# Fused window attention and MLP on one core: first loads and w_out products re-placed, and 512-token blocks in slots 72 to 135

## The chip, the core and the metric

The kernel runs on one core of one Trainium2 chip. The metric is the device time of one execution in microseconds. Four runs of the kernel before the change took 308.22 to 309.41 us, median 309.25 us. The profile shown here belongs to one execution that took 309.22 us.

## The reference

Two stages follow each other. First, attention with a window of 32 positions to each side, for 8 batches, 8 heads, 576 positions and a head dimension of 64:

```python
scores = scale * np.matmul(q, k.transpose(0, 1, 3, 2))
mask = np.abs(pos[:, None] - pos[None, :]) <= window
attn = softmax(np.where(mask, scores, -1e9))        # over the last axis
x = np.matmul(attn, v).transpose(0, 2, 1, 3).reshape(B * S, H * D)
```

This gives x with 4608 tokens (8 x 576) of 512 values. Second, an MLP with a smooth ReLU, w_in being 512 x 2048 and w_out 2048 x 512:

```python
h = x @ w_in
g = np.where(h >= 1, h, np.where(h <= -1, 0.0, (h + 1) ** 2 / 4))
out = g @ w_out
```

Inputs and output are float32 in HBM. The kernel computes with bf16 operands and float32 sums.

## The kernel before, in words

**Slots.** The MLP is cut into 18 blocks of 256 tokens (`TB`), and each block into 8 steps of 256 columns of w_in. One block and one step make one *slot*, so there are 144 slots, numbered `a`, and 8 more in which only products with w_out are left. The loop at L491 writes out the order of the work by hand; there is no scheduler (`tc.manual_schedule()`). An engine executes its instructions in the order in which this loop emits them.

One slot emits, in this order:

- `project` (L483 to L488): 8 matmuls on TensorE, each with a moving operand of 256 tokens of xT and 128 x 128 weights of w_in, into one PSUM tile `hp` of 2 x 256. Two such tiles exist (pool `ps_h`), so the matmuls of slot a wait until slot a-2 has let its tile go. Slot 6 alone takes its tile from another pool.
- ScalarE: `rr` = relu(0.5 h + 0.5) from `hp` (L519).
- VectorE: `mx` = max(hp, rr) (L526), and then `g` = min(rr, 1) * mx (L527), which goes as bf16 to a tile `gT` of this block. After `mx` the `hp` tile is free. In the slots of `two_on_act` (1 and 7 to 12) ScalarE makes the square, and VectorE reads `hp` in its single step (L524), so there the tile is free only after `g`.
- `flush` and `run(a)`: a session of the attention, if the table `sl` (L409) puts one into this slot. A session has `sums` (L265; products of probabilities with v and with ones on TensorE, then Ln and Exp on ScalarE at L299 and L300 for the reciprocal, and in the next slot a multiplication on VectorE that writes xT, L305 or L308) and `scores` or `scores8` (products of q and k on TensorE, Exp on ScalarE at L235 or L260, mask on VectorE at L201).
- w_out products: from slot 18 on `quarter` (L425), 4 matmuls with a moving operand of 512 columns of w_out (L445), on values of `gT` that are 8 slots old. Four quarters finish 128 tokens; ScalarE copies them to `osb` (L450) and SP's queue stores them. The first two blocks are done by `pair` (L453; 8 matmuls with 256 columns each, L461), in the slots that the list `pairs` (L379) names. The last 128 tokens go in two halves (L434).

**Sessions and blocks.** Batch b fills tokens 576 b to 576 b + 575 of x. A batch takes five sessions: two for its tokens 0 to 223, two for 224 to 479, and a tail session for 480 to 575. Each must be done before the first block that reads its tokens. xT is a ring of four batches.

**First loads.** POOL's queue carries all loads but the first q. They come in the order in which L118 to L157 emit them, and the loads go round over eight semaphores: the ninth waits on POOL until the first has landed, and so on. w_in comes in pieces of 256 columns, halved by rows (h = 0, 1), except for columns 1024 to 1535, which come as one piece per half. Slot a of block 0 reads columns 256 a to 256 a + 255 of both halves. `step` is made on POOL (L131) and gives, on VectorE, the identity for the transposes and the band (L138 to L140). The mask tiles are copied on POOL (L151 to L154) between the last piece of w_in and the second piece of w_out. VectorE uses them in slot 16 for the first time.

Of the kernel before, what the change touches and what calls it, by code (L numbers as in the profile page):

```python
# [7 lines left out]
FP = mybir.dt.float32  # L8
BF = mybir.dt.bfloat16
# [5 lines left out]
def kernel(  # L15
# [19 lines left out]
    nc = tc.nc  # L35
    B, H, S, D = q.shape
    NT, DM, DFF = out.shape[0], 512, 2048
# [4 lines left out]
    TAIL = S - MAIN  # L42
    RING = 4 * S
    PAD = 32
    LONG = 2

    const = ctx.enter_context(tc.tile_pool(name="const", bufs=1))
# [2 lines left out]
    ptp = ctx.enter_context(tc.tile_pool(name="ptp", bufs=2))  # L50
    smp = ctx.enter_context(tc.tile_pool(name="smp", bufs=2))
    ewp = ctx.enter_context(tc.tile_pool(name="ewp", bufs=3))
    gtp = ctx.enter_context(tc.tile_pool(name="gtp", bufs=3))
    osp = ctx.enter_context(tc.tile_pool(name="osp", bufs=3))
    ps_h = ctx.enter_context(tc.tile_pool(name="ps_h", bufs=2, space=bass.MemoryType.PSUM))
    ps_s = ctx.enter_context(tc.tile_pool(name="ps_s", bufs=1, space=bass.MemoryType.PSUM))
# [11 lines left out]
    w_in = const.tile([128, 4, DFF], BF, name="w_in")  # L68
    w_out = const.tile([128, 16, DM], BF, name="w_out")
    xT = const.tile([128, NY, RING], BF, name="xT")  # L70
    qTs = [const.tile([128, PAD + NY * S], BF, name=f"qT{i}") for i in range(3)]

    ctx.enter_context(tc.manual_schedule())
# [27 lines left out]
    def load_v(b, n):  # L101
        if b not in vn:
            vn[b] = nat.tile([128, 2 * NC, 2, D], BF, name="vn", tag="vn", bufs=3)
        h, a = divmod(n, 2)
        y = NY * h + 2 * a
        nc.gpsimd.dma_start(out=vn[b][64 * a:64 * a + 64, :, h], in_=v[b, y:y + 2].rearrange("y s d -> (y s) d")  # L106
                            .rearrange("(c r) d -> r c d", r=64))
# [14 lines left out]
    for h in range(2):  # L122
# [5 lines left out]

    step = early.tile([128, 257], BF, name="step")
    V.memset(step, 0.0)  # L130
    P.affine_select(out=step, in_=step, compare_op=ALU.is_ge, fill=-1.0, base=-65, channel_multiplier=-1,  # L131
                    pattern=[[1, 257]])
    for n in range(4):
        load_v(0, n)
    V.memset(ones, 1.0)
    for t in qTs:
# [5 lines left out]
    def put(todo):  # L142
        for fn, *x in todo:
            fn(*x)

    w = [(load_w_in, c, c + 256, h) for c in range(0, 1024, 256) for h in range(2)]
    w += [(load_w_in, 1024, 1536, h) for h in range(2)]
    w += [(load_w_in, c, c + 256, h) for c in range(1536, DFF, 256) for h in range(2)]
    put(w[:4] + [(load_half, 1, t, h) for t in range(2) for h in range(2)] + w[4:12])
    put([(load_w_out, 0, 0, 4)] + w[12:])  # L150
    P.tensor_copy(band[HD[1], 0:128], band[HD[1], 64:192])  # L151
    for m, n, x in ((mask4, 8, 128), (mask8, 4, TAIL)):
        P.tensor_copy(m.rearrange("p (n j) -> p n j", n=n),
                      band[:, :x].rearrange("p (n j) -> p n j", n=1).to_broadcast([128, n, x]))  # L154
    put([(load_w_out, 0, k, k + 4) for k in range(4, 16, 4)] + [(load_rows, 1, t) for t in range(2)])
    put([(load_v, 1, n) for n in range(4)] + [(load_w_out, 1, 8 * n, 8 * n + 8) for n in range(2)])
    put([(load_nat, 2, t) for t in range(2)] + [(load_v, 2, n) for n in range(4)])  # L157


# [156 lines left out]
    TB = 256  # L316
# [59 lines left out]

    NB = NT // TB
    NF = DFF // 256
    pairs = [(6, 0), (7, 1), (9, 2), (10, 3), (11, 4), (12, 5), (15, 6), (15, 8), (16, 7), (17, 9)]  # L379
    two_on_act = (1, 7, 8, 9, 10, 11, 12)  # L380
    ev = {}

# [23 lines left out]
        at(a, seq[2 + n][0])  # L406
    for n, a in enumerate((18, 20, 26.5, 28)):
        at(a, seq[3 + n][1])
    sl = [30, 32, 35, 39, 42, 45, 49, 52, 56, 59, 62, 65, 69, 73, 77, 81, 84, 88, 92]  # L409
    sl += [96, 99, 103, 106, 110, 113, 116, 120, 124, 128]  # L410
    for n, a in enumerate(sl):
        at(a, seq[6 + n][0], seq[7 + n][1] if n < len(sl) - 1 else None)
    for t in range(2):
# [6 lines left out]
        for t in range(2):  # L420
            xps.setdefault(a + 6 + 2 * t, []).append((b, t))

    gT, op = {}, {}

    def quarter(x):  # L425

        tt, ff = divmod(x, 4)
        if tt == NT // 128 - 1:
            half, n = divmod(ff, 2)
            if n == 0:  # L430
                op[tt] = ps_o.tile([128, 256], FP, name="op", tag="op")
            cols = slice(256 * half, 256 * half + 256)
            for j in range(NF * n, NF * n + NF):
                nc.tensor.matmul(op[tt], gT[tt // 2][:, j, 128 * (tt % 2):128 * (tt % 2) + 128], w_out[:, j, cols],  # L434
                                 start=j == 0, stop=j == 2 * NF - 1)
            if n:
                osb = osp.tile([128, 256], FP, name="osb")
                A.copy(osb, op[tt])
                nc.sync.dma_start(out=out[128 * tt:128 * tt + 128, cols], in_=osb)
            return  # L440
        if tt not in op:
            op[tt] = ps_o.tile([128, DM], FP, name="op", tag="op"), []
        o, done = op[tt]
        for j in range(4 * ff, 4 * ff + 4):
            nc.tensor.matmul(o, gT[tt // 2][:, j, 128 * (tt % 2):128 * (tt % 2) + 128], w_out[:, j],  # L445
                             start=not done, stop=len(done) == 2 * NF - 1, skip_group_check=True)
            done.append(j)
        if len(done) == 2 * NF:
            osb = osp.tile([128, DM], FP, name="osb")
            A.copy(osb, o)  # L450
            nc.sync.dma_start(out=out[128 * tt:128 * tt + 128, :], in_=osb)

    def pair(x):  # L453

        half, p, g = x // 8, x % 8 // 4, x % 4
        if (half, p) not in op:
            op[half, p] = ps_o.tile([128, 2, 256], FP, name="op", tag="op"), []
        o, done = op[half, p]
        for tt in range(2):
            for j in range(4 * g, 4 * g + 4):  # L460
                nc.tensor.matmul(o[:, tt], gT[p][:, j, 128 * tt:128 * tt + 128], w_out[:, j, 256 * half:256 * half + 256],  # L461
                                 start=not done, stop=len(done) == 4 * NF - 1, skip_group_check=True)
                done.append(j)
        if len(done) == 4 * NF:
            osb = osp.tile([128, DM], FP, name="osb")
            A.copy(osb, o.rearrange("p t f -> p (t f)"))
            nc.sync.dma_start(out=out[256 * p:256 * p + 256, 256 * half:256 * half + 256]
                              .rearrange("(t p) f -> p t f", p=128), in_=osb.rearrange("p (t f) -> p t f", t=2))
# [14 lines left out]
    def project(hp, f, r0, todo, first, last):  # L483

        for n, (j, kk) in enumerate(todo):
            nc.tensor.matmul(hp[:, j], w_in[:, kk, 256 * f + 128 * j:256 * f + 128 * j + 128],  # L486
                             xT[:, kk, r0:r0 + TB], start=first and n == 0, stop=last and n == len(todo) - 1,
                             skip_group_check=True)  # L488

    hps = []  # L490
    for a in range(NF * NB + NF):  # L491
        t, f = divmod(a, NF)
        eng = None if a < 14 else V
        post = [x for n, x in pairs if n == a] + [a - NF] * (a >= 2 * NF + 2)
        for b, x in loads.get(a, []):
            if x < 2:
                load_nat(b, x)
            else:
                for n in range(4):
                    load_v(b, n)  # L500
        if a == 0 or a > 3:
            flush()
        if t < NB:
            if t not in gT:
                gT[t] = gtp.tile([128, 2 * NF, TB], BF, name="gT", tag="gT")
            r0 = TB * t % RING
            if a in (0,):
                hps = [ps_h.tile([128, 2, TB], FP, name="hp", tag="hp") for _ in range(2)]
                for y in range(2):
                    for n in range(2):  # L510
                        project(hps[n], f + n, r0, [(j, y + 2 * m) for j in range(2) for m in range(2)], y == 0, y == 1)
            elif not hps:
                pool, tag = (ps_o, "op") if a == 6 else (ps_h, "hp")
                hps = [pool.tile([128, 2, TB], FP, name="hp", tag=tag)]
                project(hps[0], f, r0, [(j, kk) for j in range(2) for kk in (0, 2, 1, 3)], True, True)
            hp = hps.pop(0)

            rr = ewp.tile([128, 2, TB], FP, name="rr")
            A.activation(rr, hp, AF.Relu, scale=0.5, bias=0.5)  # L519
            g = gT[t][:, 2 * f:2 * f + 2]  # L520
            mx = ewp.tile([128, 2, TB], FP, name="mx")
            if a in two_on_act:
                A.activation(mx, rr, AF.Square)  # L523
                V.scalar_tensor_tensor(g, hp, 1.0, mx, op0=ALU.max, op1=ALU.min)  # L524
            else:
                V.tensor_max(mx, hp, rr)  # L526
                V.scalar_tensor_tensor(g, rr, 1.0, mx, op0=ALU.min, op1=ALU.mult)  # L527
        flush()
        run(a)
        for x in post:  # L530
            (pair if x < 4 * 4 else quarter)(x)
        run(a + 0.5)
        for x in xps.get(a, []):
            xpose(*x)
# [30 lines left out]
```

## Time and profile before

| what | us |
|---|---|
| median of four runs | 309.25 |
| the profiled execution | 309.22 |
| its span in the profile | 307.4 |
| TensorE busy | 292.9 |
| VectorE busy | 242.1 |
| ScalarE busy | 192.7 |
| POOL busy | 77.4 |
| TensorE weight loads busy | 205.8 |

Between the span and the execution's time lie 1.8 us that no engine row covers. A line of a timeline gives the start in us from the span's start, the duration, engine, source line, operation, tiles, shapes and count; brackets at the end give the idle time ahead of the group and what ended it. A line of the view of waits gives who waited, for whom, how long in total, how many times, and the longest. Matmuls overlap each other, so a group's duration is longer than the distance from its start to the next group's. The distance between starts is what a matmul costs TensorE. A few matmul records are missing: where a group shows x3 instead of x4 and 0.16 us idle ahead of it, the first of the four has no record.

### The profile page before, as it was taken

How to read it: one execution, taken by the hardware profiler on the slowest of the kernel's cores; microseconds unless marked ns; L12 is line 12 of the kernel's file. 1: busy time of each engine (PE TensorE's matmuls, PEld its weight loads, DVE VectorE, ACT ScalarE, POOL GpSimd, SP SyncE). 2: the span in 40 equal slices, each digit the busy share in tenths (PEclk: the TensorE clock that was granted, in tenths of full speed). 3: DMA queues.
4: the chain of work that ended last, by engine and by line, in shares of the span. 5: the costliest groups of instructions: out<-in, count | busy, mean ns of one | idle time of the engine just before them, and what ended most of it. 6: DMA issues, size and time to landing. Idle time of an engine off the chain costs nothing.

```text
span 307.4 us, 8448 instructions
## 1 busy us (share of the span) xinstructions
PE 292.9 (95%) x3607; PEld 205.8 (67%) x3644; DVE 242.1 (79%) x376; ACT 192.7 (63%) x320; POOL 77.4 (25%) x92
## 2 busy tenths in 40 slices
PE   7789999999999999999999999999999999999995
PEld 3458878876666666666666666666666666666654
DVE  4278568978888888889888888889888888888760
ACT  3687886747856667566656666566676666554431
POOL 8798461027008205500460002800000000000000
PEclk9999999999999999999999999999999999999999
DMA  9999999999999997996899057990810000010111
GB/s 151 184 188 195 176 203 153 170 164 143 144 203 85 169 172 101 168 105 143 109 166 135 32 107 106 149 153 25 174 54 36 34 36 36 35 36 34 59 46 68
DMA packets 137173, 35.70 MB, mean 116 GB/s; under 512 B 122160, under 2 KB 132912, under 8 KB 137136
## 3 DMA queue, kind: packets, MB, share of 16 engines
q0 software_dynamic: 102976, 18.06, 82.6%
q1 hardware_dynamic: 34016, 16.81, 25.0%
q8 instruction: 28, 0.46, 0.6%
q10 hardware_dynamic: 144, 0.29, 0.4%
q14 instruction: 9, 0.07, 0.1%
HBM read 36.70 MB, written 9.44 MB: 150 GB/s over the span
## 4 chain that ended last, share of the span: by engine, by line
PE 88%; DMA 4%; POOL 3%; issue 2%; ACT 1%; DVE 0%; POOLq 0%; ACTq 0%
PE hp L486 39%; PE op L445 34%; PE bb L293 6%; PE op L461 4%; DMA w_in<-in_moe_w_in_dram 4%; PE bb L227 2%; PE op L434 1%; POOL vn L106 1%; POOL w_in L110 1%; PE tp L187 1%; ACT pt L235 1%; POOL kh L85 0%; DVE gT L524 0%; ACT mx L523 0%; PE bb L252 0%
## 5 line engine op out<-in xcount | busy, mean ns | idle before, releaser
L486 PE MATMUL hp<-xT,w_in 128*128 128x256 bf16 x1152 | 149.4, 273 | 3.3 <-DMA w_in<-in_moe_w_in_dram 2.5
L519 ACT ACTIVATE rr<-hp 128x512 f32<-128x512 f32 x144 | 85.6, 595 | 88.5 <-PE hp L486 88.2
L486 PEld LDWEIGHTS <-w_in 128*128 128x128 bf16 x1152 | 112.0, 98 | 42.9 <-issue 3.4
L445 PE MATMUL op<-w_out,gT 128*128 128x512 bf16 x461 | 119.6, 379 | 5.0 <-issue 4.8
L526 DVE TENSOR_TENSOR mx<-hp,rr 128x512 f32<-128x512 f32 x137 | 94.5, 690 | 31.3 <-ACT rr L519 29.1
L527 DVE SCALAR_TENSOR_TENSOR gT<-rr,mx 128x512 bf16<-128x512 f32 x137 | 95.3, 695 | 4.7
L445 PEld LDWEIGHTS <-gT 128*128 128x128 bf16 x496 | 46.1, 98 | 34.8
L98 POOL DMA_DIRECT2D qn<-in_q_dram x12 | 14.6, 1222 | 113.3 <-DMA kT<-kn 109.2
L235 ACT ACTIVATE pt<-bb 128x1024 bf16<-128x1024 f32 (+1 forms) x33 | 32.7, 1002 | 4.8 <-PE bb L227 3.4
L305 DVE TENSOR_TENSOR xT<-bb,rc 128x512 bf16<-128x512 f32 (+1 forms) x32 | 21.1, 658 | 10.1 <-ACT rc L300 9.5
L106 POOL DMA_DIRECT2D vn<-in_v_dram x32 | 27.5, 893 | 4.2 <-DMA w_out<-in_moe_w_out_dram 3.3
L300 ACT ACTIVATE rc<-lr 128x512 f32<-128x512 f32 (+2 forms) x40 | 23.5, 588 | 1.3
L450 ACT COPY osb<-op 128x512 f32<-128x512 f32 x31 | 18.1, 583 | 8.7 <-PE op L445 8.3
L299 ACT ACTIVATE lr<-bb 128x512 f32<-128x512 f32 (+2 forms) x40 | 22.0, 551 | 0.4 <-PE bb L293 0.3
L201 DVE TENSOR_TENSOR pt<-pt,mask 128x1024 bf16<-128x1024 bf16 (+1 forms) x33 | 20.3, 614 | 0.5 <-ACT pt L235 0.5
L293 PE MATMUL bb<-pt,ones 64*64 64x256 bf16 (+3 forms) x352 | 19.5, 255 | 0.1
L293 PE MATMUL bb<-pt,vn 64*64 64x128 bf16 (+3 forms) x712 | 18.4, 204 | 0.1
L293 PEld LDWEIGHTS <-vn 64*64 64x64 bf16 x712 | 16.7, 107 | 0.3 <-DMA vn<-in_v_dram 0.3
L461 PE MATMUL op<-w_out,gT 128*128 128x256 bf16 x128 | 16.5, 273 | 0.0
L293 PEld LDWEIGHTS <-ones 64*64 64x64 bf16 x352 | 10.3, 105 | 8.4 <-issue 8.4
L98 POOL DMA_DIRECT2D kn<-in_k_dram x12 | 14.6, 1232 | 0.5 <-issue 0.3
L227 PE MATMUL bb<-qT,kT 64*64 64x128 bf16 (+1 forms) x520 | 13.1, 217 | 0.3 <-DVE kT L190 0.2
(59 smaller groups left out, 111.8 us busy)
## 6 DMA issues: line engine op xcount, KB each, us to landing
out_dram<-osb SPq DMA_DIRECT2D x35, 256.0 KB, 2.4
vn<-in_v_dram POOLq DMA_DIRECT2D x32, 144.0 KB, 10.1
qn<-in_q_dram POOLq DMA_DIRECT2D x12, 288.0 KB, 7.4
kn<-in_k_dram POOLq DMA_DIRECT2D x12, 288.0 KB, 9.1
w_in<-in_moe_w_in_dram POOLq DMA_DIRECT2D x12, 128.0 KB, 5.9
w_out<-in_moe_w_out_dram POOLq DMA_DIRECT2D x4, 256.0 KB, 7.1
w_out<-in_moe_w_out_dram POOLq DMA_DIRECT2D x2, 512.0 KB, 14.9
kh<-in_k_dram POOLq DMA_DIRECT2D x4, 144.0 KB, 5.3
```

The costliest lines, as they stand in the source:

```text
L98: nc.gpsimd.dma_start(out=x[:, :, h], in_=src[b, NY * h:NY * h + NY].rearrange("y s d -> (y s) d") .rearrange("(u p) d -> p u d", p=128))
L106: nc.gpsimd.dma_start(out=vn[b][64 * a:64 * a + 64, :, h], in_=v[b, y:y + 2].rearrange("y s d -> (y s) d") .rearrange("(c r) d -> r c d", ...
L235: A.activation(p, ps[:, :, :w * n].rearrange(like, y=m), AF.Exp, scale=D ** -0.5)
L293: nc.tensor.matmul(bb[HD[h], a, o + c0:o + c1], ones[HD[a]] if c is None else vn[b][HD[a], c, h], p(a, h), start=n == 0, stop=True, skip_g ...
L299: A.activation(lr[:, :, :D0], bb[:, :, D0:2 * D0], AF.Ln)
L300: A.activation(rc[:, :, :D0], lr[:, :, :D0], AF.Exp, scale=-1.0)
L445: nc.tensor.matmul(o, gT[tt // 2][:, j, 128 * (tt % 2):128 * (tt % 2) + 128], w_out[:, j], start=not done, stop=len(done) == 2 * NF - 1, s ...
L461: nc.tensor.matmul(o[:, tt], gT[p][:, j, 128 * tt:128 * tt + 128], w_out[:, j, 256 * half:256 * half + 256], start=not done, stop=len(done ...
L486: nc.tensor.matmul(hp[:, j], w_in[:, kk, 256 * f + 128 * j:256 * f + 128 * j + 128], xT[:, kk, r0:r0 + TB], start=first and n == 0, stop=l ...
L519: A.activation(rr, hp, AF.Relu, scale=0.5, bias=0.5)
L526: V.tensor_max(mx, hp, rr)
L527: V.scalar_tensor_tensor(g, rr, 1.0, mx, op0=ALU.min, op1=ALU.mult)
```

## The change

It has two parts.

**Early part.** The first load of v goes out ahead of the instruction that makes `step`. w_in is cut differently: columns 1024 to 1279 become a piece of their own, and 1280 to 1791 become the double piece. The three mask copies on POOL move behind the remaining w_out pieces of the first half, the rows of batch 1 and its v. The third and the fourth group of w_out products (`pairs`) move from slots 9 and 10 to slots 8 and 9.

**Wide part.** `gT` becomes one constant tile with four places of 256 tokens. In slots 72 to 135 two neighbouring blocks are taken together: one slot then does 128 columns of w_in for 512 tokens, with 4 matmuls of a 512-token moving operand in place of 8 with 256. A pair of blocks takes 16 slots. Its values are complete only after 16 slots, so the w_out products must fall behind: from slot 40 to slot 87 a slot gets 4, 3, 3 of them in turn (`unit`, one matmul each), from slot 88 on 4, and after the last slot 16 slots have products alone. The sessions in `sl` come earlier, so that the tokens of both blocks are ready at the start of a pair. The tail session of the fifth batch is in slot 68 (before: 73), and the last session is in slot 123 (before: 128).

```diff
+    gT = const.tile([128, 16, 4, 256], BF, name="gT")
...
+    load_v(0, 0)
     P.affine_select(out=step, in_=step, compare_op=ALU.is_ge, fill=-1.0, base=-65, channel_multiplier=-1,
                     pattern=[[1, 257]])
-    for n in range(4):
+    for n in range(1, 4):
         load_v(0, n)
...
-    w = [(load_w_in, c, c + 256, h) for c in range(0, 1024, 256) for h in range(2)]
-    w += [(load_w_in, 1024, 1536, h) for h in range(2)]
-    w += [(load_w_in, c, c + 256, h) for c in range(1536, DFF, 256) for h in range(2)]
+    cuts = [0, 256, 512, 768, 1024, 1280, 1792, DFF]
+    w = [(load_w_in, c0, c1, h) for c0, c1 in zip(cuts, cuts[1:]) for h in range(2)]
     put(w[:4] + [(load_half, 1, t, h) for t in range(2) for h in range(2)] + w[4:12])
     put([(load_w_out, 0, 0, 4)] + w[12:])
+    put([(load_w_out, 0, k, k + 4) for k in range(4, 16, 4)] + [(load_rows, 1, t) for t in range(2)])
+    put([(load_v, 1, n) for n in range(4)])
     P.tensor_copy(band[HD[1], 0:128], band[HD[1], 64:192])
     for m, n, x in ((mask4, 8, 128), (mask8, 4, TAIL)):
         P.tensor_copy(m.rearrange("p (n j) -> p n j", n=n),
                       band[:, :x].rearrange("p (n j) -> p n j", n=1).to_broadcast([128, n, x]))
-    put([(load_w_out, 0, k, k + 4) for k in range(4, 16, 4)] + [(load_rows, 1, t) for t in range(2)])
-    put([(load_v, 1, n) for n in range(4)] + [(load_w_out, 1, 8 * n, 8 * n + 8) for n in range(2)])
+    put([(load_w_out, 1, 8 * n, 8 * n + 8) for n in range(2)])
...
-    pairs = [(6, 0), (7, 1), (9, 2), (10, 3), (11, 4), (12, 5), (15, 6), (15, 8), (16, 7), (17, 9)]
+    pairs = [(6, 0), (7, 1), (8, 2), (9, 3), (11, 4), (12, 5), (15, 6), (15, 8), (16, 7), (17, 9)]
...
-    sl = [30, 32, 35, 39, 42, 45, 49, 52, 56, 59, 62, 65, 69, 73, 77, 81, 84, 88, 92]
-    sl += [96, 99, 103, 106, 110, 113, 116, 120, 124, 128]
+    sl = [30, 32, 35, 39, 42, 45, 49, 52, 55, 57, 60, 63, 66, 68, 72, 76, 79, 82, 86]
+    sl += [90, 93, 96, 100, 104, 108, 111, 114, 118, 123]
...
+    def home(t):
+        return (3 - t % 4 if t % 4 in (0, 3) else t % 4) if WIDE[0] <= NF * t < WIDE[1] else t % 4
...
+        nc.tensor.matmul(op[tt], gT[:, j, home(tt // 2), 128 * (tt % 2):128 * (tt % 2) + 128], w_out[:, j],
+                         start=j == 0, stop=j == 15)
...
+    done = 4 * (40 - NF)
+    for a in range(NF * NB + 2 * NF):
+        wide = WIDE[0] <= a < WIDE[1]
...
+        post = [] if a >= 40 else [x for n, x in pairs if n == a] + [a - NF] * (a >= 2 * NF + 2)
...
+                hp = ps_h.tile([128, 2, TB], FP, name="hp", tag="hp")
+                for n, kk in enumerate((0, 2, 1, 3)):
+                    nc.tensor.matmul(hp.rearrange("p n t -> p (n t)"), w_in[:, kk, 128 * f:128 * f + 128],
+                                     xT[:, kk, r0:r0 + 2 * TB], start=n == 0, stop=n == 3)
+                g = gT[:, f, home(t):home(t + 1) + 1:home(t + 1) - home(t)]
...
+        if a >= 40:
+            n = (4, 3, 3)[a % 3] if a < 88 else 4
+            for x in range(done, done + n):
+                unit(x)
+            done += n
```

More of the change, by code (lines that the diff above doesn't have):

```diff
@@ L44 @@
     PAD = 32
+    WIDE = 72, 136
     LONG = 2
@@ L52 @@
     ewp = ctx.enter_context(tc.tile_pool(name="ewp", bufs=3))
-    gtp = ctx.enter_context(tc.tile_pool(name="gtp", bufs=3))
     osp = ctx.enter_context(tc.tile_pool(name="osp", bufs=3))
@@ L421, with unit @@
             xps.setdefault(a + 6 + 2 * t, []).append((b, t))
-    gT, op = {}, {}
-    def quarter(x):
-        tt, ff = divmod(x, 4)
+    op = {}
+    def home(t):
+        return (3 - t % 4 if t % 4 in (0, 3) else t % 4) if WIDE[0] <= NF * t < WIDE[1] else t % 4
+    def unit(x):
+        tt, j = divmod(x, 16)
         if tt == NT // 128 - 1:
-            half, n = divmod(ff, 2)
+            half, n = divmod(j, 8)
             if n == 0:
@@ L432, in quarter @@
             cols = slice(256 * half, 256 * half + 256)
[L433 to L436, printed above, removed]
+            for k in (2 * n, 2 * n + 1):
+                nc.tensor.matmul(op[tt], gT[:, k, home(tt // 2), 128 * (tt % 2):128 * (tt % 2) + 128], w_out[:, k, cols],
+                                 start=k == 0, stop=k == 15)
+            if n == 7:
                 osb = osp.tile([128, 256], FP, name="osb")
@@ L440, in quarter @@
             return
[L441 to L448, printed above, removed]
+        if j == 0:
+            op[tt] = ps_o.tile([128, DM], FP, name="op", tag="op")
+        nc.tensor.matmul(op[tt], gT[:, j, home(tt // 2), 128 * (tt % 2):128 * (tt % 2) + 128], w_out[:, j],
+                         start=j == 0, stop=j == 15)
+        if j == 15:
             osb = osp.tile([128, DM], FP, name="osb")
-            A.copy(osb, o)
+            A.copy(osb, op[tt])
             nc.sync.dma_start(out=out[128 * tt:128 * tt + 128, :], in_=osb)
@@ L460, in pair @@
             for j in range(4 * g, 4 * g + 4):
-                nc.tensor.matmul(o[:, tt], gT[p][:, j, 128 * tt:128 * tt + 128], w_out[:, j, 256 * half:256 * half + 256],
+                nc.tensor.matmul(o[:, tt], gT[:, j, p, 128 * tt:128 * tt + 128], w_out[:, j, 256 * half:256 * half + 256],
                                  start=not done, stop=len(done) == 4 * NF - 1, skip_group_check=True)
@@ L490 @@
     hps = []
-    for a in range(NF * NB + NF):
-        t, f = divmod(a, NF)
+    done = 4 * (40 - NF)
+    for a in range(NF * NB + 2 * NF):
+        wide = WIDE[0] <= a < WIDE[1]
         eng = None if a < 14 else V
-        post = [x for n, x in pairs if n == a] + [a - NF] * (a >= 2 * NF + 2)
+        post = [] if a >= 40 else [x for n, x in pairs if n == a] + [a - NF] * (a >= 2 * NF + 2)
         for b, x in loads.get(a, []):
@@ L502 @@
             flush()
[L503 to L516, printed above, removed]
+        if a < NF * NB:
+            if wide:
+                n, f = divmod(a - WIDE[0], 2 * NF)
+                t = WIDE[0] // NF + 2 * n
+                r0 = TB * t % RING
+                hp = ps_h.tile([128, 2, TB], FP, name="hp", tag="hp")
[3 more added lines that the diff above has]
+                g = gT[:, f, home(t):home(t + 1) + 1:home(t + 1) - home(t)]
+            else:
+                t, f = divmod(a, NF)
+                r0 = TB * t % RING
+                if a in (0,):
+                    hps = [ps_h.tile([128, 2, TB], FP, name="hp", tag="hp") for _ in range(2)]
+                    for y in range(2):
+                        for n in range(2):
+                            project(hps[n], f + n, r0, [(j, y + 2 * m) for j in range(2) for m in range(2)], y == 0, y == 1)
+                elif not hps:
+                    pool, tag = (ps_o, "op") if a == 6 else (ps_h, "hp")
+                    hps = [pool.tile([128, 2, TB], FP, name="hp", tag=tag)]
+                    project(hps[0], f, r0, [(j, kk) for j in range(2) for kk in (0, 2, 1, 3)], True, True)
+                hp = hps.pop(0)
+                g = gT[:, 2 * f:2 * f + 2, home(t)]
@@ L518 @@
             rr = ewp.tile([128, 2, TB], FP, name="rr")
             A.activation(rr, hp, AF.Relu, scale=0.5, bias=0.5)
-            g = gT[t][:, 2 * f:2 * f + 2]
             mx = ewp.tile([128, 2, TB], FP, name="mx")
@@ L530 @@
         for x in post:
-            (pair if x < 4 * 4 else quarter)(x)
+            if x < 16:
+                pair(x)
+            else:
+                for j in range(4):
+                    unit(4 * x + j)
+        if a >= 40:
[3 more added lines that the diff above has]
+            done += n
         run(a + 0.5)
```

## The prediction

> **What bounds the kernel now.** I read the page's busy shares first, then TensorE's waits, then the timelines around those waits, then the chain. TensorE is busy for 95% of the span. From its waits:
>
> ```profile
> PE op L445 <- issue: 4.8, 30, 0.2
> PE hp L486 <- DMA w_in<-in_moe_w_in_dram: 2.5, 3, 0.9
> PE hp L486 <- DVE xT L305: 0.5, 1, 0.5
> PE hp L486 <- DVE gT L524: 0.3, 1, 0.3
> ```
>
> The first line is no wait. Each of its 30 idles of 0.16 us stands ahead of a group of three where four were issued; it is a missing record. The others all lie before 31.1 us; in the timeline each has a place:
>
> ```profile
> 22.05 0.29 PE L293 MATMUL bb<-pt,vn 64*64 64x32 bf16 x12
> 23.26 1.03 PE L486 MATMUL hp<-xT,w_in 128*128 128x256 bf16 x8 [0.92 <-DMA w_in<-in_moe_w_in_dram]
> ...
> 24.75 1.05 PE L486 MATMUL hp<-xT,w_in 128*128 128x256 bf16 x8
> ...
> 27.91 1.04 PE L486 MATMUL hp<-xT,w_in 128*128 128x256 bf16 x8
> 28.78 1.04 PE L461 MATMUL op<-w_out,gT 128*128 128x256 bf16 x8
> 29.65 1.04 PE L486 MATMUL hp<-xT,w_in 128*128 128x256 bf16 x8
> 31.02 1.03 PE L486 MATMUL hp<-xT,w_in 128*128 128x256 bf16 x8 [0.33 <-DVE gT L524]
> ```
>
> Slot 4 (23.26) waits for weights, slot 9 (31.02) for its PSUM tile; slots 5, 7 and 8 (24.75, 27.91, 29.65) wait for nothing. From 45 us on TensorE runs without a gap: slots without a session start 1.74 us apart, to the last one. So after 45 us only less TensorE work can save time, and any new wait of TensorE costs its full length.
>
> **Wide part, matmuls.** The chain's end has both sizes, each in a row:
>
> ```profile
> 296.23 4.32 PE op L445 x20
> 300.54 3.51 PE op L434 x32
> ```
>
> That is 216 ns for 512 columns and 110 ns for 256. Over all neighbours after 45 us, starts lie 109.3 ns apart after a 256-token matmul of L486 (mean) and 215.8 ns after a 512-column one of L445 (median 216). A wide slot costs 4 x 215.8 = 863 ns where it cost 8 x 109.3 = 874 ns: 11.2 ns saved, 64 times, **-0.72 us**. By the chain's rows, 8 x 110 - 4 x 216 = 16 ns, it would be 1.0; by groups that start 0.867 us after one another, 0.2. These are the ends. The 256 weight loads that go (98 ns each) were hidden beside the matmuls and give nothing. VectorE's `g` now goes to two pieces of 256, which costs nothing by the nearest row: the xT product (L305), which writes such pieces, takes 0.69 us as `g` does.
>
> [...]
>
> **Early part, w_in.** The landings of the loads in the trace: columns 768 to 1023 complete at 19.60 us, the double piece 1024 to 1535 at 20.87 and 23.12, 1536 to 1791 at 23.82 and 24.48. A piece takes 0.66 us behind the one before, a double piece 1.3: they queue in the DMA engines. The second double half took 2.25, 0.94 too much; a 16 KB packet of the instruction queue occupies a DMA engine from 21.84 for 0.89 us. With the new cut slot 4's weights land at 19.60 + 2 x 0.66 = 20.9, and its wait of 0.92 goes: it starts at 22.34. What is late next are slot 5's weights, now in the double piece. The bytes up to column 1791 are the same and so is the packet, so they land at 24.48 again. Slot 4 and its session are through at about 23.8; slot 5 starts at 24.48 + 0.14 (a matmul starts 0.13 to 0.14 us after the landing it waits for, at 14.80, 18.37 and 23.26) = 24.62. It started at 24.75. So of 0.92 us **-0.13** is left: the wait moves from slot 4 to slot 5. Slot 6 uses the same piece; slot 7's weights land at 27.19 and are wanted at 27.8.
>
> **Early part, the rest.** Three edits come to 0; the last line is a bound.
> - v before `step`: on POOL `step` (2.59) comes one v issue, 0.87 us, later, and with it VectorE's ident, band, bias and memsets, which ended at 4.06. VectorE then idled 1.06 us for q until its cast at 5.12; that covers it, with 0.2 to spare, and without the cover it would cost up to 0.9. The other loads are issued no sooner. Landing v earlier could help slots 0 and 1 at most by 0.24 (their xT is ready at 14.56, they start on w_in at 14.80), and slot 2 waits for w_in anyway (18.24).
> - Mask copies: they held POOL from 20.03 to 22.3. The w_out pieces behind them are issued up to 2.3 us sooner, but land 1.32 to 1.35 us apart (28.51, 29.85, 31.20) behind a load at 27.19, each one's own transfer time: the queue decides. The second half of w_out is issued about 2 us later, and landed 14 to 16 us after issue (44.47, 47.20) in the same queue. The masks are done at about 32.5 and first used after 47.5. No wait of TensorE lies here, so no gain either.
> - `pairs`: slot 7's tile is free 3.11 us after its start (27.91 to 31.02). Before, slot 9 starts 3.11 after slot 7, and slot 11 after two more slots and two groups, 4 x 0.874: 6.61 (measured 6.60). After, slot 9 comes 4 x 0.874 = 3.50 after slot 7, without a wait, but then slot 10 has no group, and slot 11 waits for slot 9's tile, 3.11: again 6.61. The wait of 0.33 becomes one of about 0.5 at slot 11. Ends: -0.37 and +0.1.
> - Bound of the w_in edit: all of the 0.92, should slot 5's piece land by 23.7.
>
> **Wide part, the lag.** The products are the same in number; each of the 16 last slots is 0.86 us of TensorE alone, on values long ready, and the last half ends in the same copy and store. The price lies in slots 40 to 87. Any three slots in a row now hold 10 products, not 12, 0.432 us less, and ScalarE and VectorE must free the tiles that much faster. A tile is free 2.40 us after its slot's start and wanted two slots later, at 3.48; of this margin of 1.08 at least 0.65 stays. The tightest place is three slots after a session: there 0.73 to 0.91 is left before, and 0.46 where the copy `osb` falls into the session's slot (59 and 99). The worst one is the session in slot 103:
>
> ```profile
> 222.91 0.63 ACT L300 ACTIVATE rc<-lr 128x512 f32<-128x512 f32 x1
> 223.45 0.57 ACT L450 COPY osb<-op 128x512 f32<-128x512 f32 x1
> 223.91 0.60 ACT L519 ACTIVATE rr<-hp 128x512 f32<-128x512 f32 x1
> ```
>
> ```profile
> 224.55 0.69 DVE L526 TENSOR_TENSOR mx<-hp,rr 128x512 f32<-128x512 f32 x1 [0.28 <-ACT rr L519]
> ```
>
> `mx` of slot 104 ends at 225.24, slot 106 starts at 225.59: 0.35 us. After the change 0.432 comes off. Margins without a copy stay at 0.30 or more, those with one become about 0.03, and the kind of slot 103 -0.08. Counting out the products, `osb` meets sessions in slots 49, 63 and 68; 49 and 63 are of the kind of 103. So **+0.16 us**; ends 0 and 0.6 (the three of them at 0.2). By distances between starts in the two timelines (VectorE: 1.33 a slot, 1.2 a session; TensorE: 0.874 + 10/3 x 0.216 a slot, 0.8 a session), 20 slots with 7 sessions (52 to 71) take VectorE 20 x 1.33 + 7 x 1.2 = 35 us and TensorE 20 x 1.59 + 7 x 0.8 = 37 us: it is not the bound, but near.
>
> **Sum**, against the profiled execution: 309.22 - 0.13 - 0.72 + 0.16 = **308.5 us**; that execution is 0.03 below the median 309.25. A measurement of this kernel can tell about 0.3%, 0.93 us, from no change: 308.3 and below is faster.
>
> **Rivals.**
> - *The early waits really go.* For it: the packet of 0.89 us could meet another transfer, then slot 5's weights land by 23.6. Against: the same bytes in the same queue. Then -0.92 for w_in, -0.72, and +0.1: 307.7 us.
> - *A new wait takes over in slots 40 to 87.* The margins of 0.03 to 0.5 are single-slot sums; sessions two slots apart (55 and 57, 66 and 68) and 93% of VectorE can carry lateness from one session into the next. It decides from the point where a tile is released later than 5.6 us after the session slot's start (5.38 and 5.56 before, without and with a copy). With 15 sessions in the stretch and 0.2 us each, 3.0 less 0.85: 311.4 us, slower. Against: VectorE is level again two slots after every session of the trace.
> - *Nothing comes of it*: wide slots save only 0.2, and slot 11's wait and the sessions take it back: 309.2 us. It belongs to the same-time cases.
>
> **How the numbers follow.** Forecast 308.5 with its ends (308.0 to 309.3): 0.58, of which 0.16 lies below 308.3. Early waits gone: 0.24. New wait: 0.11. Nothing: 0.07. Faster 0.16 + 0.24 = 0.40, same 0.42 + 0.07 = 0.49, slower 0.11. The range from 307.5 to 309.6 leaves out the new wait and a little at the other end.
>
> **What would show it.** Right: slot 4 starts at about 22.3, slot 5 at 24.6 with a wait for w_in, slot 11 with a wait of about 0.5 for VectorE; wide slots 1.727 us apart after slot 88; two waits below 0.1 at slots 52 and 66. Wrong: slot 5 without a wait; TensorE waiting for VectorE (L526) in many slots from 40 to 87; or matmuls of 512 tokens whose starts are not 216 ns apart.

## The result, and the profile after

The changed kernel takes 308.29 us (median of 46 runs, 307.81 to 308.76). The kernel before takes 308.66 us in the 73 runs beside it (308.01 to 309.66). The ratio is 0.9983, with a 95% interval of 0.9978 to 0.9988: some 0.52 us less. The means, 308.26 and 308.78, lie that far apart; the medians differ by 0.37 only, because the runs before spread more: 25 of the 73 are above 309 us, none of the 46 after. The four runs shown before the prediction lay high in this wider set: their median is 0.59 above that of the 73. The profiled execution after took 308.33 us, its span is 306.6 us; 309.22 and 307.4 stood for the kernel before.

TensorE's waits in the changed kernel (who waited, for whom, us in total, times, longest):

```profile
PE hp L489 <- DMA w_in<-in_moe_w_in_dram: 1.4, 2, 0.7
PE hp L489 <- DVE xT L307: 0.7, 2, 0.5
PE hp L489 <- DVE gT L537: 0.3, 1, 0.3
```

The same three stood there before. The one for w_in has fallen from 2.5 (three waits) to 1.4 (two), and its largest from 0.9 to 0.7; the one for xT has risen from 0.5 (one wait) to 0.7 (two), since at 14.8 us TensorE now waits for xT where it waited for w_in. Where the largest wait for w_in is now, the timeline of TensorE shows (start, duration, group; slots 4, 5, 7, 9, 10 and 11):

```profile
22.00 1.05 PE L489 MATMUL hp<-xT,w_in 128*128 128x256 bf16 x8
...
24.28 1.03 PE L489 MATMUL hp<-xT,w_in 128*128 128x256 bf16 x8 [0.71 <-DMA w_in<-in_moe_w_in_dram]
...
27.42 1.04 PE L489 MATMUL hp<-xT,w_in 128*128 128x256 bf16 x8
...
30.91 1.04 PE L489 MATMUL hp<-xT,w_in 128*128 128x256 bf16 x8
...
32.66 1.04 PE L489 MATMUL hp<-xT,w_in 128*128 128x256 bf16 x8
34.02 1.03 PE L489 MATMUL hp<-xT,w_in 128*128 128x256 bf16 x8 [0.33 <-DVE gT L537]
```

Slot 4 no longer waits; slot 5 does. Slot 9 no longer waits; slot 11 does. From slot 7 to slot 11 it is 6.60 us, as before the change. A stretch of the wide part, between two sessions:

```profile
184.50 1.03 PE L514 MATMUL hp<-xT,w_in 128*128 128x512 bf16 x4
185.36 1.03 PE L449 MATMUL op<-w_out,gT 128*128 128x512 bf16 x4
186.22 1.03 PE L514 MATMUL hp<-xT,w_in 128*128 128x512 bf16 x4
```

A wide slot is 1.72 us from start to start, in two halves of 0.86. The starts of the slots cut both executions into stages. The stages from slot 11 on are the same to 0.02 us in every kernel below that has the same code there, with one exception (slots 11 to 40 in e11); the stage ahead of slot 11 differs from execution to execution. Differences are taken before rounding.

| stage (us) | before | after | difference |
|---|---|---|---|
| span's start to slot 11 | 34.51 | 34.02 | -0.48 |
| slot 11 to slot 40 | 61.78 | 61.77 | -0.01 |
| slots 40 to 71 | 62.92 | 59.18 | products put off |
| slots 72 to 135 | 123.82 | 120.27 | products put off, wide |
| slots 136 to 142 | 12.16 | 12.16 | 0 |
| slot 143 to the last matmul | 8.57 | 15.48 | the products put off |
| slot 11 to the last matmul | 269.26 | 268.86 | **-0.39** |

### The profile page after: what moved, and what is told of

The parts are those of the page before. It is cut to its first block, busy times and chain, and to the rows that moved or that the text cites. A ratio compares the mean times of both kernels' runs of the same rounds, so it can differ in the third digit from the quotient of the medians.

```text
span 306.6 us, 7936 instructions
## 1 busy us (share of the span) xinstructions
PE 292.7 (95%) x3350; PEld 181.0 (59%) x3388; DVE 240.2 (78%) x376; ACT 191.5 (62%) x320; POOL 76.9 (25%) x92
## 4 chain that ended last, share of the span: by engine, by line
PE 88%; DMA 4%; POOL 3%; issue 2%; ACT 1%; DVE 0%; POOLq 0%; ACTq 0%
PE op L449 34%; PE hp L489 21%; PE hp L514 18%; PE bb L295 6%; PE op L464 4%; DMA w_in<-in_moe_w_in_dram 2%; PE bb L229 2%; DMA qh<-in_q_dram 2%; POOL w_in L111 1%; PE op L440 1%; POOL vn L107 1%; PE tp L189 1%; ACT pt L237 1%; POOL kh L86 0%; DVE gT L537 0%
## 5 line engine op out<-in xcount | busy, mean ns | idle before, releaser
L539 DVE TENSOR_TENSOR mx<-hp,rr 128x512 f32<-128x512 f32 x137 | 94.4, 689 | 25.7 <-ACT rr L533 23.9
L489 PE MATMUL hp<-xT,w_in 128*128 128x256 bf16 x640 | 83.1, 273 | 2.5 <-DMA w_in<-in_moe_w_in_dram 1.4
L489 PEld LDWEIGHTS <-w_in 128*128 128x128 bf16 x640 | 61.9, 98 | 22.8 <-issue 3.0
L514 PE MATMUL hp<-xT,w_in 128*128 128x512 bf16 x256 | 65.7, 379 | 0.0
L514 PEld LDWEIGHTS <-w_in 128*128 128x128 bf16 x256 | 25.0, 98 | 30.2
L453 ACT COPY osb<-op 128x512 f32<-128x512 f32 x31 | 18.0, 580 | 11.4 <-PE op L449 11.1
L302 ACT ACTIVATE rc<-lr 128x512 f32<-128x512 f32 (+2 forms) x40 | 23.5, 587 | 1.3
L464 PE MATMUL op<-w_out,gT 128*128 128x256 bf16 x128 | 16.5, 273 | 0.0
```

The costliest lines, as they stand in the source:

```text
L302: A.activation(rc[:, :, :D0], lr[:, :, :D0], AF.Exp, scale=-1.0)
L464: nc.tensor.matmul(o[:, tt], gT[:, j, p, 128 * tt:128 * tt + 128], w_out[:, j, 256 * half:256 * half + 256], start=not done, stop=len(done ...
L514: nc.tensor.matmul(hp.rearrange("p n t -> p (n t)"), w_in[:, kk, 128 * f:128 * f + 128], xT[:, kk, r0:r0 + 2 * TB], start=n == 0, stop=n == 3)
```

## The experiments

The kernel before took 308.5 to 308.8 us (medians) beside these runs. Every ratio is to it.

**e7_lag** separates the two parts of the wide part. It keeps the lag and the new places of the sessions, but no slot is wide:

```diff
-    WIDE = 72, 136
+    WIDE = 160, 160
```

> The changed kernel without any 512-token block: the same later products, the same sessions, the same early part, but 8 matmuls of 256 tokens in each slot. My theory: the 64 slots are 11 ns longer again, 0.72 us slower than the changed kernel, ratio to before about 1.0007, with the waits at slots 52 and 66 kept. Rival (the matmul size gives nothing, the gain comes from the later products or the denser sessions): ratio to before 0.998 to 0.9985, as the changed kernel.

Measured: 308.84 us, ratio 1.0006 (0.9996 to 1.0016). From slot 11 to the last matmul it takes 269.52 us: 0.26 more than before, 0.65 more than the changed kernel. Of the 0.65, 0.64 lies in slots 72 to 135 (120.91 against 120.27). The same stretch as above, in e7:

```profile
184.34 1.04 PE L489 MATMUL hp<-xT,w_in 128*128 128x256 bf16 x8
185.21 1.03 PE L449 MATMUL op<-w_out,gT 128*128 128x512 bf16 x4
186.07 1.04 PE L489 MATMUL hp<-xT,w_in 128*128 128x256 bf16 x8
```

Eight matmuls of 256 take 0.87 us, four of 512 in the fence above 0.86. So the 512-token matmuls alone are worth 0.64 us, 10 ns a slot, and the lag with its sessions costs 0.26.

**e4_sessions** asks where the 0.26 comes from. In the changed kernel the slots 49 and 63 hold a session and the copy `osb`. Two sessions move one slot earlier, and nothing else:

```diff
-    sl = [30, 32, 35, 39, 42, 45, 49, 52, 55, 57, 60, 63, 66, 68, 72, 76, 79, 82, 86]
+    sl = [30, 32, 35, 39, 42, 45, 48, 52, 55, 57, 60, 62, 66, 68, 72, 76, 79, 82, 86]
```

> The changed kernel with two sessions moved one slot earlier, from 49 to 48 and from 63 to 62, so that the copy of a finished output tile no longer falls into their slots. My theory: the waits of 0.13 us at slots 52 and 66 go and none comes, 0.26 us faster than the changed kernel, ratio to before about 0.9975. Rival (VectorE and ScalarE carry their lateness from session to session): sessions 60 and 62 now lie two slots apart and a new wait of 0.1 to 0.3 us stands after slot 62, no gain, ratio to before about 0.9983 or above.

Measured: 307.93 us, ratio 0.998 (0.9969 to 0.9991). The ratio alone can't be told from the changed kernel's 0.9983, but the stage can: slots 40 to 71 take 58.93 us where the changed kernel takes 59.18. The timelines show how. First TensorE, ScalarE and VectorE of the changed kernel, behind the session in slot 49:

```profile
115.71 1.04 PE L489 MATMUL hp<-xT,w_in 128*128 128x256 bf16 x8
116.58 1.03 PE L449 MATMUL op<-w_out,gT 128*128 128x512 bf16 x4
117.58 1.03 PE L489 MATMUL hp<-xT,w_in 128*128 128x256 bf16 x8
```

```profile
115.20 0.63 ACT L302 ACTIVATE rc<-lr 128x512 f32<-128x512 f32 x1
115.74 0.57 ACT L453 COPY osb<-op 128x512 f32<-128x512 f32 x1
116.20 1.18 ACT L533 ACTIVATE rr<-hp 128x512 f32<-128x512 f32 x2
```

```profile
116.84 0.69 DVE L539 TENSOR_TENSOR mx<-hp,rr 128x512 f32<-128x512 f32 x1 [0.28 <-ACT rr L533]
```

Four products of 216 ns from 116.58 end at 117.44, but slot 52 (third line) starts at 117.58. What it waits for is `mx`, done at 116.84 + 0.69 = 117.53; `mx` waited for `rr`, and `rr` stood behind `rc` and the copy on ScalarE. The waits view doesn't show this one, since the products' recorded end, 116.58 + 1.03 = 117.61, lies past that start; the distance between starts does. In e4 the copy and the session are in different slots, and the same three groups are:

```profile
115.52 1.04 PE L489 MATMUL hp<-xT,w_in 128*128 128x256 bf16 x8
116.39 1.03 PE L449 MATMUL op<-w_out,gT 128*128 128x512 bf16 x4
117.25 1.04 PE L489 MATMUL hp<-xT,w_in 128*128 128x256 bf16 x8
```

There it is 1.73 us from slot 51 to slot 52, and 1.87 in the changed kernel. Slot 66 shows the same: 1.52 against 1.65. These two waits of 0.13 us are the whole price of the lag: with both gone, e4 takes 268.62 us from slot 11 to the last matmul, 0.64 less than the kernel before, which is what the matmuls give. Counted from the starts, no other slot from 40 to 142 of the changed kernel takes over 0.03 us more than its own matmuls and its session (0.52 to 0.90 us, as before). So session 68, the third that the prediction counted out, costs nothing.

**e1_early** puts the early part alone into the kernel before (the edits of the early part in the diff above, and no others), **e2_wide** the wide part alone.

> The kernel before with the early part alone (v load ahead of step, new cut of w_in, mask copies later, two products one slot earlier). My theory: the wait of 0.92 us at slot 4 goes and most of it comes back at slot 5, and the stall of slot 9 moves to slot 11; so 0.15 to 0.3 us faster than before, ratio about 0.9992. Rival A (the early part is the whole gain, the wide part nets nothing): 0.5 us faster, ratio about 0.9983. Rival B (the wide part is the whole gain): no change, ratio 1.0000.

> The changed kernel with the early part undone: 512-token blocks, later w_out products, earlier sessions alone. My theory: 64 slots shorter by 11 ns (0.72 us) less two waits of 0.13 us at slots 52 and 66, so 0.46 us faster than before, ratio about 0.9985, with slot 4 waiting 0.9 us for w_in as before. Rival A (early part is the whole gain): ratio 1.0000. Rival B (the wide part is the whole gain): ratio about 0.9983.

Measured: e1 308.60 us, 0.9995 (0.9984 to 1.0006). e2 308.48 us, 0.9986 (0.9972 to 1.0). The wide part has most of the gain; the early part, some 0.15 us with an interval from -0.5 to +0.2, can't be told from nothing. Multiplied, the two ratios give 0.9981; the whole is 0.9983. From slot 11 on e2 has the stages of the changed kernel (268.87 us in all) and e1 those of the kernel before (269.25), so there the wide part's gain of 0.39 is sure.

**e5_cuts** gives the kernel before only the new cut of w_in, **e6_vfirst** only the first load of v ahead of `step`.

```diff
-    w = [(load_w_in, c, c + 256, h) for c in range(0, 1024, 256) for h in range(2)]
-    w += [(load_w_in, 1024, 1536, h) for h in range(2)]
-    w += [(load_w_in, c, c + 256, h) for c in range(1536, DFF, 256) for h in range(2)]
+    cuts = [0, 256, 512, 768, 1024, 1280, 1792, DFF]
+    w = [(load_w_in, c0, c1, h) for c0, c1 in zip(cuts, cuts[1:]) for h in range(2)]
```

> The kernel before with the new cut of w_in alone. My theory: it is the whole of what the early part gives: slot 4 without a wait, slot 5 with one of 0.5 to 0.8 us, 0.15 to 0.3 us faster than before, ratio about 0.9992. Rival (the gain of the early part lies in the other three edits): ratio 1.0000.

> The kernel before with the first v load ahead of step alone. My theory: VectorE's later start is covered by its wait for q (0.14 us to spare) and slot 2 waits for w_in at 18.24 us in any case; no change, ratio 1.0000. Rival A (v lands sooner, the loads behind it follow): 0.2 to 0.4 us faster. Rival B (the later step reaches the first transposes): up to 0.4 us slower.

Measured: e5 308.66 us, 0.9997 (0.9989 to 1.0006), runs from 308.1 to 308.9. e6 308.38 us, 0.9995 (0.9982 to 1.0007), runs from 308.1 to 309.6. Neither can be told from the kernel before. In the profiled executions the second half of the double piece landed this long after the first (a double piece alone is 1.3): with the old cut 2.25 us before, 2.05 in e2 and 1.27 in e6; with the new cut 1.88 after, 1.79 in e7, 1.75 in e5, 1.71 in e4 and 1.27 in e1. In e6, with the old cut and a punctual half, slot 4 waits only 0.21 us and slot 5 starts at 23.68; in e1, with the new cut and a punctual half, slot 5 starts at 23.60. So where the half is punctual the cut gains almost nothing. Where it is late, slot 5 waits in place of slot 4, and slot 7 starts at 27.09 to 27.44 (the changed kernel, e4, e5, e7) instead of 27.70 and 27.91 (e2 and before). The runs of a kernel spread less without the old cut: their standard deviation is 0.21 to 0.31 us in the changed kernel, e1, e3, e4, e5, e7 and e8, and 0.45 to 0.56 in the kernel before, e2 and e6. (In e9 and e11 below it is 0.56 to 0.57 without the old cut, so the cut is not all that decides it.) That the late half makes this spread is argued: only one execution of each kernel has a trace.

**e3_pieces** cuts w_in of the changed kernel into single pieces throughout, **e8_both** adds e4's sessions.

```diff
-    cuts = [0, 256, 512, 768, 1024, 1280, 1792, DFF]
+    cuts = list(range(0, DFF + 1, 256))
...
-    put(w[:4] + [(load_half, 1, t, h) for t in range(2) for h in range(2)] + w[4:12])
-    put([(load_w_out, 0, 0, 4)] + w[12:])
+    put(w[:4] + [(load_half, 1, t, h) for t in range(2) for h in range(2)] + w[4:14])
+    put([(load_w_out, 0, 0, 4)] + w[14:])
```

> The changed kernel with the double piece 1280 to 1791 cut into two pieces of 256 columns as well, two loads more. My theory: slot 5 waits only because its 256 columns come in the double piece behind 512 columns; cut, they land 1.3 us sooner or more (near 22.3 to 22.9 us instead of 24.15), the wait of 0.71 us at slot 5 goes and no other takes its place, since slot 6 is then wanted at about 25 us: 0.7 us faster than the changed kernel, ratio to before about 0.996. Rival (the DMA queue is the limit whatever the cut, and each further load costs 0.6 us of POOL and a turn of the eight semaphores): slot 5's or slot 6's weights land as late as now or later, ratio to before 0.998 or above.

> The changed kernel with both further edits: w_in in pieces of 256 columns throughout, and sessions 48 and 62 in place of 49 and 63. My theory: both waits go, 0.7 and 0.26 us, about 1 us faster than the changed kernel, ratio to before about 0.995. Rival (slot 5's weights come no sooner, or the waits move on): ratio to before 0.998.

Measured: e3 308.07 us, 0.9982 (0.9972 to 0.9993): not to be told from the changed kernel's 0.9983, where 0.7 us were expected. TensorE's timeline of e3 from slot 5 on (the view ends at 34 us, so its last line has four of slot 11's eight matmuls):

```profile
23.44 1.05 PE L489 MATMUL hp<-xT,w_in 128*128 128x256 bf16 x8
...
26.74 1.04 PE L489 MATMUL hp<-xT,w_in 128*128 128x256 bf16 x8
27.69 1.03 PE L464 MATMUL op<-w_out,gT 128*128 128x256 bf16 x8
28.56 1.04 PE L489 MATMUL hp<-xT,w_in 128*128 128x256 bf16 x8
29.59 1.03 PE L464 MATMUL op<-w_out,gT 128*128 128x256 bf16 x8
...
33.58 0.60 PE L489 MATMUL hp<-xT,w_in 128*128 128x256 bf16 x4 [0.33 <-DVE gT L537]
```

The wait of slot 5 has gone: its weights landed at 22.19. But the groups of L464 now start 0.95 and 1.03 us after the slot's matmuls, not 0.87: the w_out pieces behind them landed at 27.64 and 29.55, and the group waits for each. Slot 7 is 0.68 us earlier than in the changed kernel, slot 11 only 0.44. e8 took 307.75 us (307.52 to 308.29), 0.9969 (0.9957 to 0.998): the best kernel here, by its ratio some 0.95 us below the kernel before. From slot 11 on its stages are e4's, so the sessions bring a sure 0.25 of it. What its pieces add to e4 (0.9969 against 0.998) lies within the intervals.

**e9, e10 and e11** test why the second half was late. The prediction blamed a 16 KB packet of the instruction queue. The trace before has 28 of these packets beside 7251 TensorE instructions, the trace after 26 beside 6738: one to 259 in both. 156 more TensorE instructions ahead of the attention are 0.6 of such a step; the author's estimate was that they move the one at 21.84 away, and that in e9 the wait of slot 5 falls from 0.7 to 0.1 us or less, for a ratio of 0.9973. The 11 idle matmuls that keep TensorE busy at the start become 89 shorter ones, on the changed kernel (e9), the one before (e10) and e8 (e11).

```diff
-    def keep_warm(n, pool, tag):
+    def keep_warm(n, pool, tag, w=512):
...
-            nc.tensor.matmul(z, warm[:, :128], warm, start=True, stop=True)
+            nc.tensor.matmul(z[:min(w, 128), :w], warm[:, :min(w, 128)], warm[:, :w], start=True, stop=True)
...
-        keep_warm(11, ps_h, "hp")
+        keep_warm(89, ps_h, "hp", 64)
```

> The changed kernel with its first 11 warming matmuls of 512 columns replaced by 89 of 64 columns: 156 TensorE instructions more before the work begins, about the same time. [...] Rival (the late landings come from the load queue itself): slot 5's weights land between 23.4 and 24.2 as before, ratio about 0.9983.

> The kernel before with the same 156 TensorE instructions more. My theory: the packets that made the second half of the double piece land at 23.1 instead of 22.1 us come at other times, slot 4's wait falls from 0.92 to about 0.2 us, and the runs above 309 us, nearly half of those of the kernel before, go: median about 308.3, ratio 0.999. Rival (the late landings come from the load queue itself): the runs spread from 308.0 to 309.6 as before, ratio 1.000.

> The changed kernel with all three further edits: w_in in pieces of 256 columns, sessions in slots 48 and 62, and the 156 TensorE instructions more. My theory: with no packet in the way the w_out pieces that the groups of slots 7 and 8 wait for land up to 0.9 us sooner too; 0.2 to 0.4 us faster than without the instructions, ratio to before about 0.996. Rival (the packets do not matter): ratio about 0.9969 as without them.

Measured: e9 308.67 us, 1.0001 (0.9987 to 1.0015). e10 309.58 us, 1.0024 (1.0012 to 1.0036). e11 308.63 us, 0.9996 (0.9983 to 1.0009). All three are slower than the kernels they came from. The packets moved as meant. In e9's trace the half then came 1.39 us after the first, and slot 5 has no wait in the waits view, as estimated; but e10 and e1 contradict it. In e10 slot 4 still waits, and longer, with no instruction packet near: here is its timeline, and then the queues of e10 from 15.6 to 23.9 us (packets, MB, share of 16 engines), in which the instruction queue has no line:

```profile
23.94 1.03 PE L486 MATMUL hp<-xT,w_in 128*128 128x256 bf16 x8 [1.05 <-DMA w_in<-in_moe_w_in_dram]
```

```profile
q0 software_dynamic: 2383, 1.43, 128.2%
```

The second half landed 2.36 us after the first. The other way round, e1 has the packet in the middle of its double piece (queues from 21.6 to 23.2 us):

```profile
q0 software_dynamic: 471, 0.30, 129.8%
q8 instruction: 1, 0.02, 3.5%
```

It starts at 21.93, takes 0.89 us, and the half came punctually, 1.27 us after the first. So the packet is neither needed for a late half nor enough for one. What e10 shows instead are a few load packets of 0.5 to 1 KB that took 0.41 to 0.60 us each (median 0.06); in the execution before some took 0.28 to 0.31, in e6 none over 0.12. But these are not the whole answer either: the changed kernel and e5 had a late half with no load packet over 0.14 and an instruction packet in it (from 22.12 and 22.14). What makes the half late stays open, and it may have more than one cause. Why the three are slower is seen mostly in their first 15 us: the first instruction packet comes at 7.5 to 8.1 us instead of about 12.5, among the first loads, and takes 1.5 to 1.7 us; the first piece of w_in lands at 12.5 to 12.7 (11.4 to 11.8 without the edit), slot 0 starts at 14.5 to 14.7 (13.3 to 13.7). At slot 11 the delay is 0.7 us in e9 and e10 and 0.2 in e11, which loses another 0.3 in slot 14 (2.44 us, 2.15 in e8), where no wait is listed. That the packet causes this delay, and not the matmuls themselves, wasn't separated.

## Why the prediction was right, step by step

The time was forecast at 308.5 us and is 308.29; the change was forecast at -0.69 us, of which 0.52 was found. By terms:

| term (us) | predicted | measured |
|---|---|---|
| 512-token matmuls | -0.72 | -0.64 (after against e7) |
| lag and sessions | +0.16 | +0.26 (e7 against before) |
| early part | -0.13 | -0.15, -0.5 to +0.2 (e1) |
| sum | -0.69 | -0.53; by the ratio -0.52 |

- **The level.** The sum was made against an execution of 309.22, 0.56 above the median of 73 runs. With that median it would have given 307.97, 0.32 too low; from the high execution it came out 0.21 too high. So that the time was met so closely is partly luck. The profiled pair differs by 0.89, of which 0.48 lies ahead of slot 11, where the prediction had 0.13. Of this 0.48, 0.27 is there at slot 3 already (20.32 before, 20.05 after), where the prediction had nothing. The fourth load of w_in (columns 256 to 511, second half) landed at 14.66 before and at 13.58 after; ScalarE and VectorE came to the first two slots 0.45 us later, and so the weight loads for the products of q and k ahead of slot 3 waited 0.35 us for kT. First before, then after (PEld are TensorE's weight loads):

```profile
19.05 0.70 DVE L190 COPY kT<-tp 128x512 bf16<-128x512 bf16 x1
...
19.80 0.26 PEld L227 LDWEIGHTS <-kT 64*64 64x64 bf16 x16 [0.35 <-DVE kT L190]
```

```profile
18.60 0.70 DVE L192 COPY kT<-tp 128x512 bf16<-128x512 bf16 x1
...
19.35 0.43 PEld L229 LDWEIGHTS <-kT 64*64 64x64 bf16 x16
```

This landing varies too: 13.40 to 13.83 in e1, e4, e6 and e8, 14.32 to 14.61 in e2, e3, e5 and e7. All the early ones load v first, but so do e3 and e7; whether that edit has a share in it stays open.
- **Matmuls.** Right, slightly too large: 10 ns a slot where 11.2 was worked out from distances between starts. The chain's end (16 ns) and the groups (0.2 us in all) were worse rows. The 256 weight loads that went were hidden, as said: weight loads are busy for 59% of the span after 67%, and it bought nothing. The changed kernel's 512-token starts are 215.8 to 216 ns apart, as predicted.
- **Lag.** The two places are those that were named, slots 52 and 66, by the mechanism that was named (`rr` behind the copy, then `mx`). Each is 0.13 us and not 0.08: the room of 0.35 us was read at slot 106 of the kernel before and carried over to slots 52 and 66, and there it fell 0.05 us short of that. The rival of a new wait throughout slots 40 to 87 fell with the first trace: but for the two, no slot there is late.
- **w_in.** Slot 4 came at 22.00 (22.34 predicted) and slot 5, waiting for its weights, at 24.28 (24.62): the wait moved. The step that failed is its reason. "The bytes up to column 1791 are the same and so is the packet" gave the landing at 24.48; it was 24.15, and 23.5 to 24.2 in e1, e4, e5 and e7, which have the same cut. The late half varies from execution to execution, and the packet alone doesn't decide it (e10, e1). So the early waits do go sometimes (e1's slot 5 starts at 23.60), which was put as a rival of its own; but then the old cut loses little too (e6), so that the rival's 0.92 is not there either.
- **v ahead of `step`.** Right. On VectorE of the changed kernel (start, duration):

```profile
3.92 0.23 DVE L140 TENSOR_TENSOR ident<-step 128x128 bf16<-128x128 bf16 x1 [2.36 <-POOL step L133]
...
4.81 0.11 DVE L354 MEMSET kT<- 128x64 uint32 x1
5.06 0.79 DVE L344 CAST qb<-q 128x640 bf16<-128x640 f32 x1
```

`ident` waits 2.36 us for POOL, but the memsets still end ahead of the cast, at 4.92, with 0.14 to spare. A wait of 2.4 us in the list costs nothing here.
- **`pairs` and masks.** Right: 6.60 us from slot 7 to slot 11, and nothing waits for a mask. Slot 11 starts 1.36 us after slot 10 where 0.87 was due, so it loses the 0.5 predicted; the view lists 0.33 of it. But slot 9 before lost as much (1.37 after slot 8, 0.33 listed): the prediction set a listed wait beside a distance between starts, and the wait moved without growing.

## What to carry to other kernels

Where TensorE is busy for 95% of the span, count the distances between starts in the stretch itself: a larger moving operand saved 10 ns in 0.87 us, and the many weight loads that went with it nothing. Ahead of an edit that lets less TensorE work pass per step, look for steps in which two rare jobs of another engine coincide, and place them apart: that alone gave back 0.25 us (e4). A profiled execution is one draw: compare stages, take those that repeat to 0.02 us as they are, and those that follow early transfers only from many runs.

## What the runs showed of the hardware beyond that

Transfers of the same bytes in the same order landed up to a microsecond apart in executions of different kernels: the second half of the double piece came 1.27 to 2.36 us after the first with the old cut, and 1.27 to 1.88 with the new one in four kernels that have the same loads (e1, e4, e7 and the changed kernel). A wait of 0.13 us between matmuls need not stand in the waits view: it was found only as 1.87 us between two starts where 1.73 was due. The 28 instruction packets of 16 KB in the trace before took 0.88 to 1.83 us, 15 of them under 1.0; the first ones of e9, e10 and e11, which came at 7.5 to 8.1 us, took 1.5 to 1.7.
